# Splitting the last 1 KB of one key/value load unevenly, and joining four loads of output weights into two

## The chip, the cores and the metric

The kernel runs on one core of one Trainium2 chip. The metric is the time on the device in microseconds, of which the median over several executions is taken. A profile belongs to one execution; its span runs from the first to the last instruction of the program, and the execution's own time is a little longer.

## The reference

One decoding step for 8 sequences mixes two branches with a gate: `g * a + (1 - g) * b`, where `g = sigmoid(sum(x * gate_w))`.

Branch `a` is attention over the last 1024 positions of a cache, with 16 query heads over 8 key/value heads of 256 elements:

```
q = x @ wq                              # 8 x 4096, 16 heads of 256
p = softmax(q . k * 256**-0.5)          # each pair of query heads shares one key/value head
a = (p . v) @ wo                        # wo is 4096 x 448
```

Branch `b` is a layer norm, a matrix 448 x 1792 with bias and GELU, and a matrix 1792 x 448 with bias. All inputs are bfloat16. The keys and values of the window are by far the most of what has to be read: 16 groups of 2 MB each for the keys and as much for the values, out of 77.7 MB in all.

## The kernel before, in words

The cache is worked on in 16 groups (`NQ`), each of one sequence and four key/value heads. A group's keys are one tile of 128 partitions x 8192 elements (16 KB a partition, 2 MB in all), its values another. A partition holds 32 successive positions of one head, and partition `4 s + a` belongs to block `s` of positions and head `a` of the group. So the source of a load is a view of three dimensions: `s` (32), `a` (4), and the contiguous 8192 elements.

All large loads go through one ring of nine such tiles (`RING`), and all are issued by the SP queue. `plan` is the list of loads in their order: the query weights, the keys of group 0, the weights of branch `b`, then alternately keys of group `u` and values of group `u - 2` (`LAG`), the last two groups' values, and the output weights wo. `pump()` issues the next loads as soon as a ring tile is free, and `done()` says that one is. In the compiled program each load also waits on one of eight completion semaphores that are used in turn, which means that it waits for the load eight places before it.

wo is cut into four quarters of eight rows a partition. `WO_PARTS` says in which pieces each quarter is loaded: the first two quarters in two pieces of four rows (3584 B a partition, 448 KB), the last two in pieces of four, two and two rows. Two quarters share one ring tile. `project(q)` multiplies quarter `q` and waits for the pieces that it reads.

On the engines a group passes these steps. DVE turns the keys by 32 x 32 blocks (`turn_keys`, L358), PE forms the scores (`scores`, L430), DVE and ACT do the softmax (`top`, `share`, `expo`), DVE turns the weights (`turn`, L472), PE multiplies them with the values (`values`, L502), and `gather` and `finish` put the result into `oT`. The steps of three groups overlap in an order written out by hand. At the end come the last group's values, `spread_rows`, the four `project` calls (L673), one DVE instruction that adds the two branches (L691), and three small stores (L701).

Small inputs (`x_sb`, `gw_b`, both of eight rows, and the two biases) are loaded from the ACT queue at the start.

Of the kernel before, what the change touches and what calls it, by code (L numbers as in the profile page):

```python
# [18 lines left out]
def kernel(  # L19
# [15 lines left out]
    nc = tc.nc  # L35
# [3 lines left out]
    _, Hkv, Sk, Dh = A_k_cache.shape  # L39
# [20 lines left out]
    QUAD = 4  # L60
    RQ = QUAD * rep
    NQ = NB * Hkv // QUAD
    SK = P // QUAD
    NCK = W // SK
# [4 lines left out]
    HPQ = 4  # L69
    NHQ = Hq // HPQ  # L70
    NJ8 = HPQ * NJ
    WO_PARTS = [[(0, 4), (4, 8)]] * 2 + [[(0, 4), (4, 6), (6, 8)]] * 2
    RING = 9
    LAG = 2
    NK = 4
    NPAR = 2
    KP = NK * NPAR
    BLK = 32
# [10 lines left out]
    epool = ctx.enter_context(tc.tile_pool(name="epool", bufs=2))  # L89
    opool = ctx.enter_context(tc.tile_pool(name="opool", bufs=LAG + 1))  # L90
    ps_s = ctx.enter_context(tc.tile_pool(name="ps_s", bufs=2, space=PSUM))
# [18 lines left out]
    def kv_loader(src, u, parts):  # L110
        b, half = divmod(u, Hkv // QUAD)
        v = src[b, half * QUAD : (half + 1) * QUAD, kv_base:Sk, :].rearrange(
            "a (s c) d -> s a (c d)", c=NCK
        )

        def load(t):
            n = NCK * Dh // parts
            for i in range(parts):
                nc.sync.dma_start(
                    t[:, i * n : (i + 1) * n], v[:, :, i * n : (i + 1) * n]  # L120
                )

        return load

    def rows_loader(pieces):
        def load(t):
# [15 lines left out]
    def add(key, loader):  # L142
        index[key] = len(plan)
        plan.append(loader)

    def add_kv(name, src, u, parts=1):
        add((name, u), kv_loader(src, u, parts))
# [13 lines left out]
    for u in range(1, NQ):  # L161
        add_kv("k", A_k_cache, u)
        if u >= LAG:
            add_kv("v", A_v_cache, u - LAG)
    for u in range(NQ - LAG, NQ):
        add_kv("v", A_v_cache, u)
    for q in range(0, NHQ, 2):
# [5 lines left out]
                    for i in range(2)  # L173
                    for j0, j1 in WO_PARTS[q + i]
                ]
# [3 lines left out]
    def slot(*key):  # L179
        return slots[index[key]]  # L180
# [40 lines left out]
    qw = consts.tile([P, NJ, NU, AREA], BF16)  # L221
    pick = consts.tile([P, NK // NJ, NPAR, P], BF16)
    same = consts.tile([P, P], F32)
# [60 lines left out]
    )  # L284
    for kk in range(NK // NJ):
        for par in range(NPAR):
            nc.vector.tensor_copy(
                pick[:, kk, par, :].rearrange("p (b w) -> p b w", b=QUAD),
                ident[:]
                .rearrange("p (k o w r) -> p k r o w", k=NK // NJ, o=1, r=NPAR)[:, kk, par]  # L290
                .to_broadcast([P, QUAD, BLK]),
# [62 lines left out]
    def turn_keys(u, hf):  # L354
        kn = slot("k", u)
        kt = ktpool.tile([P, CH, NK, BLK, NPAR], BF16, tag="kt", name="kt")
        KT[u, hf] = kt
# [7 lines left out]
    def query():  # L365
# [31 lines left out]
        for j in range(NJ):  # L397
            for kk in range(NK // NJ):
                for par in range(NPAR):
# [19 lines left out]
    def scores(u, hf):  # L419
        if hf == 0:  # L420
            S[u] = ps_s.tile([P, W], F32, tag="S", name="S")
        cols = slice(hf * CH * BLK, (hf + 1) * CH * BLK)
        kt = KT.pop((u, hf))
        nc.tensor.matmul(  # L424
            S[u][:, cols], lhsT=foreign[:], rhs=place[:], start=True, stop=False
        )
        for k in range(NK):
            for par in range(NPAR):
                j, m = k // (NK // NJ), k % (NK // NJ) * NPAR + par
                nc.tensor.matmul(  # L430
                    S[u][:, cols],
                    lhsT=qw[:, j, u, m * RQ : m * RQ + P],
                    rhs=kt[:, :, k, :, par],
                    start=False,
                    stop=(k == NK - 1 and par == NPAR - 1),
                )
# [77 lines left out]
    def gather(u):  # L514
        first = soft.pop(u)
        os_ = epool.tile([P, Dh], F32, tag="os", name="os_")
        nc.vector.scalar_tensor_tensor(
            os_[:],
            in0=PO[:, 1, :],
            scalar=own[:, 1:2],  # L520
            in1=first[:],
            op0=ALU.mult,
            op1=ALU.add,
        )
        soft[u] = os_
# [89 lines left out]
    for u in range(1, NQ):  # L615
        turn_keys(u, 0)
        scores(u, 0)
        if u >= LAG + 1:
            gather(u - LAG - 1)
        if u >= LAG:  # L620
# [12 lines left out]
    u = NQ - 1  # L633
# [98 lines left out]
```

## Time and profile before

| | |
|---|---|
| median of 6 runs | 190.51 us (190.34 to 190.83) |
| the profiled execution's own time | 190.68 us |
| its span | 188.9 us |
| PE busy | 128.9 us, 68% |
| DVE busy | 127.9 us, 68% |
| ACT busy | 43.3 us, 23% |
| loads of keys and of values: one | 2 MB, 36.7 and 36.8 us from issue to landing (median) |
| loads of wo | 6 of 448 KB and 4 of 224 KB |
| read from memory | 77.68 MB, 411 GB/s over the span |

How to read the views that follow: the page's second part cuts the span into 40 slices of 4.7 us, with a digit for the busy tenths of each. Its third part counts the packets of each queue: q1 is SP's, q10 ACT's, q8 and q14 bring instructions. The chain of waits goes back from the last instruction to whatever released each step; its columns are start, length and what it was. A view of stretches gives, for each window, its length, the busy time and number of instructions of PE, PE's weight loads, DVE, ACT and POOL, the granted clock of PE, the DMA share and GB/s. The trace also has a record of each packet: its queue, size, start and duration.

### The profile page before, as it was taken

What the parts mean: (1) busy time and instruction counts of PE and PEld (TensorE: products, weight loads), DVE (VectorE), ACT (ScalarE), POOL (GpSimd) and SP (SyncE); (2) the same over time, 40 slices, a digit from 0 to 9 for tenths busy, and PEclk for the clock granted to TensorE, in tenths of its full rate; (3) what the DMA queues carried; (4) which work ended last, traced back from release to release, by engine and by line L of the source; (5) the groups of instructions that cost most, each with busy time, mean ns of one, the idle gap of its engine ahead of it and who ended that gap; (6) DMA issues with size and microseconds to landing.
All of it is one profiled execution on the core that took longest, in us unless ns stands there. A gap on an engine that the chain in (4) does not pass through costs nothing.

```text
span 188.9 us, 2411 instructions
## 1 busy us (share of the span) xinstructions
PE 128.9 (68%) x966; PEld 68.3 (36%) x975; DVE 127.9 (68%) x186; ACT 43.3 (23%) x91; POOL 5.0 (3%) x7
## 2 busy tenths in 40 slices
PE   0056879897847575786669675848399849687592
PEld 0022853442414242334225333323153514244281
DVE  7840488998949494949494949495868677785300
ACT  2032310034040404040404040404004310435200
POOL 8100000000000000000000000000000000000000
PEclk9999999999999999699979999999757987999558
DMA  6999999999999999999999999999999999999990
GB/s 213 408 427 427 434 433 429 430 430 427 437 430 427 427 437 427 427 430 441 427 430 425 434 427 434 434 427 434 423 434 434 437 420 434 427 437 415 409 375 28
DMA packets 7293, 77.84 MB, mean 412 GB/s; under 512 B 993, under 2 KB 1650, under 8 KB 2546
## 3 DMA queue, kind: packets, MB, share of 16 engines
q1 hardware_dynamic: 7088, 77.67, 97.0%
q8 instruction: 7, 0.11, 0.2%
q10 hardware_dynamic: 194, 0.02, 0.1%
q14 instruction: 4, 0.03, 0.0%
HBM read 77.68 MB, written 0.01 MB: 411 GB/s over the span
## 4 chain that ended last, share of the span: by engine, by line
DMA 79%; DVE 13%; PE 4%; ACT 2%; issue 1%; SPq 0%; ACTq 0%
DMA slot<-in_A_k_cache_dram 39%; DMA slot<-in_A_wo_dram 20%; DMA slot<-in_A_v_cache_dram 19%; DVE kt L358 5%; PE Sq L372 2%; DVE xz L246 1%; ACT qw L413 1%; DVE qw L415 1%; DVE mx L442 1%; PE qt L387 1%; ACT qs L382 1%; PE qp L400 1%; DVE Sq L199 0%; DVE ET L472 0%; PE gp L343 0%
## 5 line engine op out<-in xcount | busy, mean ns | idle before, releaser
L358 DVE STREAM_TRANSPOSE kt<-slot 128x2048 int32<-128x2048 int32 x32 | 73.7, 2305 | 31.5 <-DMA slot<-in_A_k_cache_dram 31.5
L430 PE MATMUL S<-kt,qw 128*128 128x512 bf16 x256 | 69.3, 417 | 35.2 <-DVE kt L358 30.5
L430 PEld LDWEIGHTS <-qw 128*128 128x128 bf16 x256 | 26.3, 103 | 72.2 <-issue 50.9
L459 ACT ACTIVATE E<-S,nmx 128x1024 bf16<-128x1024 f32 x16 | 22.2, 1388 | 2.8 <-DVE nmx L456 2.8
L535 ACT CAST oT<-fin 128x16 bf16<-128x16 f32 x16 | 3.6, 227 | 77.5 <-PE fin L532 77.5
L502 PE MATMUL PO<-slot,ET 128*16 128x512 bf16 x256 | 18.3, 410 | 1.2 <-DMA slot<-in_A_v_cache_dram 1.2
L442 DVE TENSOR_REDUCE mx<-S 128x1 f32<-128x1024 f32 x16 | 19.0, 1185 | 0.0
L511 ACT ACTIVATE first<-PO,own 128x256 f32<-128x256 f32 x16 | 7.6, 474 | 28.1 <-PE PO L502 26.7
L472 DVE STREAM_TRANSPOSE ET<-E 128x512 int32<-128x512 int32 x16 | 11.2, 698 | 2.2 <-ACT E L459 2.2
L424 PE MATMUL S<-place,foreign 128*128 128x512 bf16 x23 | 9.2, 400 | 0.2
L450 PE MATMUL mz<-m,same 128*128 128x4 f32 x32 | 6.2, 265 | 4.2 <-ACT oT L535 4.1
L483 PEld LDWEIGHTS den<-rowsum,rowden 128*128 128x128 f32 x32 | 6.7, 215 | 3.4 <-issue 1.1
L502 PEld LDWEIGHTS <-ET 128*16 128x16 bf16 x256 | 5.3, 91 | 5.8 <-issue 2.1
L450 PEld LDWEIGHTS mz<-m,same 128*128 128x128 f32 x32 | 5.0, 195 | 6.1 <-ACT oT L535 5.3
L424 PEld LDWEIGHTS <-foreign 128*128 128x128 bf16 x32 | 3.2, 100 | 8.5 <-issue 6.7
L483 PE MATMUL den<-rowsum,rowden 128*128 128x1 f32 x32 | 5.0, 226 | 0.4 <-ACT E L459 0.4
L673 PE MATMUL A_ps<-slot,oP 128*8 128x144 bf16 (+1 forms) x96 | 4.7, 316 | 0.7 <-DMA slot<-in_A_wo_dram 0.7
L415 DVE CAST qw<-qp 32x512 bf16<-32x512 f32 x4 | 2.7, 687 | 3.4 <-ACT qw L413 3.4
L494 ACT ACTIVATE rsel<-sel,rb 128x8 f32<-128x8 f32 x16 | 4.8, 297 | 1.1 <-DVE rb L493 1.1
L293 POOL MEMSET qw<- 128x5120 bf16 x1 | 4.4, 4366 | 0.0
L391 DVE COPY qd<-qt 128x64 bf16<-128x64 bf16 x4 | 0.6, 215 | 5.5 <-PE qt L387 5.5
L673 PEld LDWEIGHTS <-oP 128*8 128x8 bf16 x96 | 3.8, 114 | 1.2 <-issue 1.1
(135 smaller groups left out, 86.5 us busy)
## 6 DMA issues: line engine op xcount, KB each, us to landing
slot<-in_A_v_cache_dram SPq DMA_DIRECT2D x16, 2048.0 KB, 36.8
slot<-in_A_k_cache_dram SPq DMA_DIRECT2D x15, 2048.0 KB, 36.7
slot<-in_A_wo_dram SPq DMA_DIRECT2D x6, 448.0 KB, 31.3
slot<-in_A_wq_dram SPq DMA_DIRECT2D x1, 2048.0 KB, 7.7
slot<-in_A_k_cache_dram SPq DMA_DIRECT2D x2, 1024.0 KB
slot<-in_B_w_dram SPq DMA_DIRECT2D x1, 1568.0 KB
slot<-in_B_w_dram SPq DMA_DIRECT2D x1, 1344.0 KB, 11.8
slot<-in_A_wq_dram SPq DMA_DIRECT2D x1, 1024.0 KB
```

The lines of the kernel that those rows point to most:

```text
L358: nc.vector.transpose(kt[:].rearrange("p c k x r -> p (c k x r)").bitcast(WORD), kn[:, hf * CH * Dh : (hf + 1) * CH * Dh].bitcast(WORD),)
L424: nc.tensor.matmul(S[u][:, cols], lhsT=foreign[:], rhs=place[:], start=True, stop=False)
L430: nc.tensor.matmul(S[u][:, cols], lhsT=qw[:, j, u, m * RQ : m * RQ + P], rhs=kt[:, :, k, :, par], start=False, stop=(k == NK - 1 and par = ...
L442: nc.vector.reduce_max(mx[:], S[u][:], axis=AXIS.X)
L450: nc.tensor.matmul(mz[:], lhsT=same[:], rhs=m4[:], start=True, stop=True)
L459: nc.scalar.activation(E[:].rearrange("p c x i -> p c i x"), S.pop(u)[:].rearrange("p (c i x) -> p c i x", i=PAIR, x=BLK), ACT.Exp, bias=n ...
L472: nc.vector.transpose(ET[:].rearrange("p c r i -> p (c r i)").bitcast(WORD), E[:].rearrange("p c x i -> p (c x i)").bitcast(WORD),)
L483: nc.tensor.matmul(den[u][:], lhsT=rowden[:], rhs=rowsum[:], start=True, stop=True)
L494: nc.scalar.activation(rsel[u][:], sel2[:], ACT.Copy, scale=rb[:])
L502: nc.tensor.matmul(PO[32 * t : 32 * t + PAIR * RQ], lhsT=ET[:, c, 0:RQ, :], rhs=vn[:, PAIR * c * Dh : PAIR * (c + 1) * Dh], start=(c < QUA ...
L511: nc.scalar.activation(first[:], PO[:, 0, :], ACT.Copy, scale=own[:, 0:1])
L673: nc.tensor.matmul(dst, lhsT=oP[:, j, q, :], rhs=w[:, o + cols.start : o + cols.stop], start=(q == 0 and j == 0), stop=(q == NHQ - 1 and j ...
```

## The change

The values of group 6 are loaded in three transfers instead of one: the first 15 KB of each of the 128 rows, then the last 1 KB (`SKEW`, 512 elements) of the first 96 rows, then that of the other 32. The first two quarters of wo are loaded in one transfer each (7168 B a partition) instead of two. All the bytes, their places and the order of everything else stay as they are; no instruction of PE, DVE, ACT or POOL is added, removed or moved, and SP issues as many transfers as before, two more in the middle and two fewer at wo.

```diff
-    WO_PARTS = [[(0, 4), (4, 8)]] * 2 + [[(0, 4), (4, 6), (6, 8)]] * 2
+    WO_PARTS = [[(0, 8)]] * 2 + [[(0, 4), (4, 6), (6, 8)]] * 2
...
+    SKEW = 512
...
-        return load
+        def load_skewed(t):
+            n = NCK * Dh - SKEW
+            nc.sync.dma_start(t[:, :n], v[:, :, :n])
+            for s0, s1 in ((0, 24), (24, SK)):
+                nc.sync.dma_start(t[QUAD * s0 : QUAD * s1, n:], v[s0:s1, :, n:])
+
+        return load if parts else load_skewed
...
-            add_kv("v", A_v_cache, u - LAG)
+            add_kv("v", A_v_cache, u - LAG, parts=0 if u == NQ // 2 else 1)
```

## The prediction

> **What bounds the kernel now.** First the occupancy and transfer part of the page.
>
> ```profile
> DMA  6999999999999999999999999999999999999990
> GB/s 213 408 427 427 434 433 429 430 430 427 437 430 427 427 437 427 427 430 441 427 430 425 434 427 434 434 427 434 423 434 434 437 420 434 427 437 415 409 375 28
> DMA packets 7293, 77.84 MB, mean 412 GB/s; under 512 B 993, under 2 KB 1650, under 8 KB 2546
> ...
> q1 hardware_dynamic: 7088, 77.67, 97.0%
> q8 instruction: 7, 0.11, 0.2%
> ```
>
> The 16 DMA engines are busy from the second slice to the last but one, at about 430 GB/s, while PE and DVE are each busy 68% of the span. Then the chain of waits in order of time, at its end:
>
> ```profile
> 110.48 36.83 DMA slot<-in_A_v_cache_dram
> 147.31 0.02 issue
> 147.33 31.34 DMA slot<-in_A_wo_dram
> 178.67 0.02 issue
> 178.69 6.95 DMA slot<-in_A_wo_dram
> 185.64 0.04 issue
> 185.68 0.33 PE A_ps L673 x6
> 186.01 0.03 issue
> 186.04 0.38 DVE res L691
> ```
>
> Each link is a load whose landing frees the semaphore for the next one. The last part of wo lands at 185.64; after it come only six matmuls, one DVE instruction and the store. So the end is the moment when the slowest DMA engine has finished. Last, the stretches of 1 us around that moment (the last two columns are the DMA share and GB/s):
>
> ```profile
> 182.00:183.00 1.00, 1.00 (x32) 1.00 (x29) 0.29 (x1) 0.00 (x0) 0.00 (x0) 0.50 1.02 393
> 183.00:184.00 1.00, 1.00 (x22) 0.77 (x15) 0.00 (x0) 0.00 (x0) 0.00 (x0) 0.50 0.79 308
> 184.00:185.00 1.00, 0.44 (x12) 0.44 (x12) 0.00 (x0) 0.00 (x0) 0.00 (x0) 0.50 0.39 150
> 185.00:186.00 1.00, 0.81 (x18) 0.35 (x12) 0.00 (x0) 0.00 (x0) 0.00 (x0) 0.82 0.02 7
> ```
>
> The engines do not end together: 0.79, then 0.39 of 16 work on while the others are done. I followed the transfer records of the trace, where on one engine each packet starts where the one before ends. That gives 16 finishing times: nine engines end between 183.65 and 184.53, six between 184.98 and 185.35, one at 185.64; the mean is 184.52. The seven late ones are exactly those that each carried one of the seven 16 KB instruction packets of q8 (at 24.9, 43.4, 74.0, 102.6, 131.7, 160.7 and 180.6 us). Such a packet sets its engine back about 1.1 us: 0.61 of its own, and about 0.5 by which the rows beside it took longer. The engine that ends last got the last packet; the runner-up, at 185.35, the first.
>
> Which engines are these? The eight that carried the eight-row load of gw_b I call low, the rest high. The runner-up is low; the last one and the other five are high. One low, then six high is what a walk through engines 7, 8, ... 13 would give, so I place the last one at 13. That is an inference; the records carry no engine number.
>
> **What the Trainium skill says.** "DMA: Bandwidth & Descriptors", section on why a DMA increments its semaphore by 16: a transfer runs on the largest k up to 16 that divides the slowest dimension of both access patterns, on the lowest-numbered k engines. The trace agrees as far as it goes: 6272 rows, 16 completion writes for each of 49 loads, and twice 8 rows with 8 writes for the stores on SP, make 7088, the packets of q1. Applied to the change: the source of the 96 rows is 24 x 4 x 512, so k = 12, eight rows on each of engines 0 to 11; that of the 32 rows is 8 x 4 x 512, so k = 8, four rows on each of 0 to 7. No transfer before has k = 12.
> Same page, "Why small descriptors are slow": about 3 cycles are lost per packet. The records agree in size: a packet follows the next after 607 ns for 16 KB, 136 for 3584 B and 70 for 1792 B, which is 0.0368 ns per byte plus 4 ns; a completion write takes 6.
> Same page, "Bandwidth": transfers under 1 MB are inefficient. Here they are not, since they lie queued back to back: the 448 KB ones lose only these 4 ns per row.
>
> **The change part by part**, per DMA engine.
> - Values of group 6: 8 rows shrink by 1 KB each: -8 x 37.7 = -302 ns everywhere. The tail costs 41.7 ns a row and 6 ns per completion write: engines 0 to 7 get 12 rows and two writes, +512; 8 to 11 get 8 rows and one write, +340; 12 to 15 nothing.
> - wo: the first two quarters become 8 + 8 rows of 7168 B in place of 16 + 16 of 3584 B: 16 packets less, -64, and two writes less, -12.
> - Sum: engines 0 to 7 **+0.135 us**, 8 to 11 **-0.038**, 12 to 15 **-0.378**.
>
> New ends: the last one 185.64 - 0.38 = 185.26; the high ones in 8 to 11 at most 185.19 - 0.04 = 185.15; the low runner-up 185.35 + 0.13 = **185.49**, now last. The end moves by 185.49 - 185.64 = **-0.16 us** (-0.155 unrounded). The 0.74 us of PE and DVE and the store behind it stay.
>
> What I cost at nothing: SP issues two transfers more (about 0.53 us each) and two fewer of wo (0.33 each). Eight semaphores are shared in turn, so each transfer waits for the one eight before it; the tails take two of the eight places, and transfers behind them on SP are issued two loads later. The median issue-to-landing time is 36.8 us, about 7.6 loads of 4.86 us; it falls to some 27, still five loads ahead, so no engine runs dry. The last wo part is issued on the landing of the last values (176.5) instead of 178.67, earlier. From group 6 to wo the low engines run 0.21 us later (512 - 302), so keys and values land that much later: the matmuls on group 6 start at 100.99, 2.3 us after its landing at 98.69, which covers its own tail; at the end the matmuls on the last values, waiting for DMA at 176.5, shift by 0.21, and PE then sits idle 0.56 us before 184.56 for a wo part, which covers it. The single semaphore of quarter 0 comes with its second half, at 178.67 as before, and PE begins it only at 180.53; quarter 1 is whole at 180.87, needed at 181.67. If that cover were gone, PE would add at most the delay beyond it. DVE waits 31.5 us in all for keys, so 0.2 us is hidden there too; POOL and ACT's queue are not touched.
>
> The profiled execution took 190.68 us, its span 188.9; the median of the runs is 190.51, 0.17 lower. I take the difference off the median: 190.51 - 0.16 = **190.35**.
>
> **Rivals.** What a measurement can tell from no change is about 0.2%, 0.38 us.
> - *Full relief.* If in most executions the low engine with the instruction packet ends well ahead (its start and the cost of its packet vary), the relieved engine's whole 0.378 us counts: 190.13, right at the 0.2% line. For it: nothing else of the low eight is later than 184.53. Against: the runner-up is here only 0.29 behind.
> - *The last engine is one of 8 to 11*, or the late ones change places between executions: -0.04, 190.47. For it: the placing is inferred.
> - *Slower: the low engine is already last.* Place: the end of wo on the low engine with an instruction packet. Price +0.135 us, 190.65. It decides once that engine ends less than 0.135 us behind the last one; here it is 0.29. The tail can cost more than the sum if twelve engines are not used: 96 rows on eight engines would make it 16 rows on each low one, +0.30 us, 185.65 and 190.52.
> - *The skew does not come about.* If both tails spread over all 16 engines, each pays 32 + 12 ns for the tails and saves 76: -0.03, 190.48.
>
> **How the numbers follow.** Main case 0.48; full relief 0.15; last engine in 8 to 11 0.17; low engine last 0.09; no skew 0.11. All but full relief stay within 0.2%; of that, half lies beyond, and I add as much again for what I have not priced, in the rows beside the small packets or in the order of the late engines: faster by over 0.2% 0.16, within 0.2% 0.77, slower by over 0.2% 0.07 (the low case with a dearer tail). The range reaches from a little below full relief, 190.05, to a little above the low case, 190.72.
>
> **What would show it.** q1 should hold 6948 packets: 7088 - 256 + 128 rows, and 32 - 20 completion writes less; with tails on all 16 engines it would be 6960. Packets under 512 B should fall from 993 to 981 (993 without skew). In the stretches around the end, the DMA share should fall to nothing some 0.16 us earlier, and the landing of the last wo part, 185.64, with it. I am wrong if the keys' waits on DVE grow by more than about 0.2 us each, if the DMA share dips after group 6, or if PE waits for quarter 0 or 1 of wo and not for the last part.

## The result: slower by a quarter of a per cent

The changed kernel takes 190.95 us (median of 20 runs, 190.64 to 191.48), the kernel before 190.48 (40 runs beside it). The ratio is 1.0025, 95% interval 1.0015 to 1.0034: +0.47 us where -0.16 was forecast. (The ratios here leave out single executions that stand far above the rest.) The profiled execution took 191.30 us, its span 189.5.

The occupancy and transfer part of the page of the changed kernel:

```profile
DMA  6999999999999999999999999999999999999990
GB/s 212 416 420 436 435 422 437 429 425 432 425 439 429 429 429 429 439 429 425 429 398 384 431 436 436 422 432 432 425 436 429 432 429 432 432 425 428 412 380 29
DMA packets 7153, 77.84 MB, mean 411 GB/s; under 512 B 981, under 2 KB 1766, under 8 KB 2406
...
q1 hardware_dynamic: 6948, 77.67, 97.1%
```

The packets are those forecast for 12 and 8 engines: 6948 on q1, and 981 under 512 B. The new thing is in the GB/s row: slices 21 and 22 (about 95 to 104 us) show 398 and 384 where the row of before had nothing below 420 between its third and its 36th slice. The DMA row keeps its nines there. So the engines don't run dry; they are busy for longer with the same bytes.

The end of the chain of waits:

```profile
177.25 0.02 issue
177.27 8.99 DMA slot<-in_A_wo_dram
186.26 0.04 issue
186.30 0.33 PE A_ps L680 x5
186.63 0.03 issue
186.66 0.38 DVE res L698
```

The last part of wo is issued at 177.27, earlier than before, as forecast, and still lands at 186.26 in place of 185.64. Six matmuls (the chain lists five of them, the trace has six), one DVE instruction and the store follow as before. The whole difference is in the landing.

The stretches of 1 us around it, with the same columns as before:

```profile
183.00:184.00 1.00, 1.00 (x32) 1.00 (x26) 0.05 (x1) 0.00 (x0) 0.00 (x0) 0.50 1.04 410
184.00:185.00 1.00, 0.76 (x16) 0.53 (x10) 0.00 (x0) 0.00 (x0) 0.00 (x0) 0.50 0.69 266
185.00:186.00 1.00, 0.64 (x18) 0.44 (x18) 0.00 (x0) 0.00 (x0) 0.00 (x0) 0.85 0.20 77
186.00:187.00 1.00, 0.39 (x12) 0.10 (x5) 0.34 (x1) 0.00 (x0) 0.00 (x0) 1.00 0.00 0
```

The DMA share falls over two stretches as before, half to one us later: the engines are late together, not one of them. Where they lost the time is seen when longer stretches are laid around the two low slices. First the kernel before, then the changed one:

```profile
85.00:97.00 12.00, 6.73 (x44) 3.43 (x45) 9.23 (x11) 2.26 (x5) 0.00 (x0) 0.98 1.01 434
97.00:100.00 3.00, 3.00 (x11) 1.71 (x9) 2.96 (x4) 0.00 (x0) 0.00 (x0) 0.50 1.01 431
100.00:103.00 3.00, 2.68 (x26) 1.37 (x26) 0.95 (x3) 1.15 (x4) 0.00 (x0) 0.99 0.99 421
103.00:115.00 12.00, 7.42 (x48) 3.56 (x47) 8.66 (x9) 3.33 (x7) 0.00 (x0) 1.00 1.01 431
```

```profile
85.00:97.00 12.00, 6.77 (x44) 3.43 (x45) 9.20 (x11) 2.25 (x5) 0.00 (x0) 0.98 1.01 431
97.00:100.00 3.00, 3.00 (x11) 1.71 (x9) 2.96 (x4) 0.00 (x0) 0.00 (x0) 0.51 1.03 378
100.00:103.00 3.00, 2.68 (x26) 1.33 (x26) 0.91 (x3) 1.16 (x4) 0.00 (x0) 1.00 0.98 366
103.00:115.00 12.00, 9.07 (x47) 4.05 (x47) 7.92 (x9) 3.30 (x7) 0.00 (x0) 0.86 1.01 429
```

For six microseconds 372 GB/s on average flow in place of 426, with PE, DVE and ACT doing the same work as before. The packet records give the detail; their times count here and below from the same zero as the views (the prediction put them 0.35 us later, so that the last one meets its landing at 185.64). The two tails, the transfers of 96 and of 32 rows of 1 KB, pass between 96.1 and 98.5 us. The slow 16 KB rows start between 96.6 and 102.8 us. They settle at 707 ns on every one of the 16 engines, also on those that carry no tail; before and after that a row takes 611, but for the rows beside an instruction packet. Added up and divided by 16, an engine loses 0.80 us there.

The engine that waits for these rows shows it too. DVE turns the keys of group 9, first before, then in the changed kernel:

```profile
103.57 2.31 DVE L358 STREAM_TRANSPOSE kt<-slot 128x2048 int32<-128x2048 int32 x1 [2.32 <-DMA slot<-in_A_k_cache_dram]
```

```profile
104.47 2.31 DVE L365 STREAM_TRANSPOSE kt<-slot 128x2048 int32<-128x2048 int32 x1 [3.25 <-DMA slot<-in_A_k_cache_dram]
```

The wait is 0.93 us longer, and all such waits together are 33.2 us in place of 31.5.

### The profile page after: what moved, and what is told of

Its sections match the earlier page's. It is cut to its first block, busy times and chain, and to the rows that moved or that the text cites. A ratio compares the mean times of both kernels' runs of the same rounds, so it can differ in the third digit from the quotient of the medians.

```text
span 189.5 us, 2411 instructions
## 1 busy us (share of the span) xinstructions
PE 129.1 (68%) x966; PEld 68.3 (36%) x975; DVE 128.1 (68%) x186; ACT 43.3 (23%) x91; POOL 5.0 (3%) x7
## 3 DMA queue, kind: packets, MB, share of 16 engines
q1 hardware_dynamic: 6948, 77.67, 97.1%
## 4 chain that ended last, share of the span: by engine, by line
DMA 91%; DVE 5%; PE 2%; issue 0%; SPq 0%
DMA slot<-in_A_k_cache_dram 57%; DMA slot<-in_A_v_cache_dram 19%; DMA slot<-in_B_w_dram 6%; DMA slot<-in_A_wo_dram 5%; DMA slot<-in_A_wq_dram 4%; DVE kt L365 4%; PE S L437 2%; DVE mx L449 1%; DVE ET L479 0%; DVE res L698 0%; DVE os__1181 L524 0%; PE A_ps L680 0%; DVE m L451 0%; PE den L490 0%; SPq L120 0%
## 5 line engine op out<-in xcount | busy, mean ns | idle before, releaser
L365 DVE STREAM_TRANSPOSE kt<-slot 128x2048 int32<-128x2048 int32 x32 | 73.7, 2305 | 33.3 <-DMA slot<-in_A_k_cache_dram 33.2
L451 DVE TENSOR_SCALAR m<-block,mx 128x4 f32<-128x4 f32 x16 | 3.7, 229 | 0.6
```

The source lines that it names most:

```text
L365: nc.vector.transpose(kt[:].rearrange("p c k x r -> p (c k x r)").bitcast(WORD), kn[:, hf * CH * Dh : (hf + 1) * CH * Dh].bitcast(WORD),)
```

## The experiments

The first four runs weigh three theories, which the expectations call by number: 1, transfers on fewer than 16 engines make the load behind them slow; 2, it is the two more transfers or the rows of 1 KB as such; 3, it is the joined loads of wo. The later ones weigh theory A, transfers over fewer than 128 rows disturb the stream (A1: because fewer than 16 engines are used, A2: because of the rows alone), against theory B, there are too few large loads in flight. All edits are to the kernel before, with constants written out; "lost" is the packets' time above the usual one of their size, from the records of the traced execution, per engine.

**One part at a time.** `skew_only` leaves the edit of `WO_PARTS` out, `wo_only` makes that edit alone:

```diff
-    WO_PARTS = [[(0, 4), (4, 8)]] * 2 + [[(0, 4), (4, 6), (6, 8)]] * 2
+    WO_PARTS = [[(0, 8)]] * 2 + [[(0, 4), (4, 6), (6, 8)]] * 2
```

> Only the split of the values of group 6 (15 KB rows, then 96 and 32 rows of 1 KB); wo is loaded as in the kernel before. Theory 1 (transfers that run on fewer than 16 DMA engines make the load behind them slow): the 16 KB rows of the keys of group 9 take about 707 ns in place of 611 on all engines, 8 x 96 = 0.77 us each, and the time is 0.4 to 0.7 us above before, 190.9 to 191.2. Theory 2 (two more transfers in the eight places, or rows of 1 KB as such): the same here. Theory 3 (the joined loads of wo are to blame): within 0.1 us of before, 190.4 to 190.6, and no slow rows.

> Only the first two quarters of wo in one transfer each. Theories 1 and 2: 16 packets and two completion writes less on each engine, -0.08 us, 190.4, no slow rows anywhere. Theory 3: slower by 0.3 us or more.

The split alone takes 1.0054 times as long (1.0033 to 1.0075), 191.65 us; wo alone 1.0006 (0.9998 to 1.0014), which is no difference that can be told. Theory 3 is out. The gain of 0.08 us that I had for wo doesn't show either. The stretches of the split alone, 97 to 100 and 100 to 103 us:

```profile
97.00:100.00 3.00, 2.70 (x16) 1.51 (x13) 2.90 (x3) 0.23 (x1) 0.00 (x0) 0.98 1.00 361
100.00:103.00 3.00, 2.98 (x26) 1.39 (x27) 0.88 (x3) 1.55 (x3) 0.00 (x0) 1.00 1.00 360
```

Here the rows settle at 732 ns, and 0.98 us are lost.

**Tails over all engines.** In the split's loader:

```diff
-            for s0, s1 in ((0, 24), (24, SK)):
+            for s0, s1 in ((0, 16), (16, SK)):     # tail_64_64
+            for s0, s1 in ((0, SK),):              # tail_128
```

> As the split alone, but the tails have 64 and 64 rows (source 16 x 4 x 512 each), so that both run on 16 engines by the rule of the skill: the same number of transfers, the same bytes, no skew. Theory 1: no slow rows, time +0.04 us (8 packets of 4 ns and 2 writes of 6 ns per engine), 190.5. Theory 2: the keys of group 9 slow as in the changed kernel, 190.9 to 191.2.

> As the split alone, but the tail is one transfer of 128 rows of 1 KB on 16 engines. Theory 1: no slow rows, 190.5. Theory 2 by number of transfers: about half the loss, 190.7; by the 1 KB rows: 190.9 to 191.2.

`tail_128`: ratio 1.0012 (0.9999 to 1.0024), no slow rows, 437 and 418 GB/s in the two stretches. So rows of 1 KB do no harm. `tail_64_64`: ratio 1.0027 (1.0013 to 1.0041), with times from 190.63 to 191.52; the traced execution, at 190.63, has a few rows of 630 to 675 ns at its tails and had lost only 0.04 us. As first put, theory 1 (fewer than 16 engines) did not foresee that the kernel is slower; so I took a second trace of it.

> The same kernel as tail_64_64, for a second execution's trace. If its times of 190.6 to 191.5 come from slow rows that appear in some executions only, an execution of 191 or more shows them here, and one of 190.7 does not.

This execution took 205.78 us. Its row of GB/s, and stretches from 85 us on:

```profile
GB/s 233 401 429 436 439 419 427 440 414 447 427 424 437 424 440 427 427 433 425 376 368 360 360 360 360 360 363 363 360 360 360 360 360 357 360 360 360 373 396 39
```

```profile
85.00:97.00 12.00, 7.93 (x51) 3.93 (x51) 9.20 (x12) 2.25 (x5) 0.00 (x0) 1.00 1.00 424
97.00:100.00 3.00, 2.68 (x29) 1.65 (x27) 2.96 (x3) 0.23 (x1) 0.00 (x0) 1.00 1.09 406
100.00:110.00 10.00, 5.78 (x22) 2.16 (x19) 6.13 (x9) 2.00 (x4) 0.00 (x0) 0.75 1.00 360
110.00:140.00 30.00, 21.95 (x116) 10.90 (x117) 15.93 (x20) 6.66 (x15) 0.00 (x0) 0.74 1.01 360
140.00:170.00 30.00, 21.08 (x120) 10.29 (x119) 20.68 (x24) 4.75 (x12) 0.00 (x0) 0.83 1.01 360
```

The fall begins as the two tails pass (96.2 to 98.3 us) and does not end: 732 ns a row to the last 16 KB row, 15.0 us lost on these rows. PE's granted clock was 1.00 as it began, so it does not come from there. The tails themselves are two microseconds long. So they don't make particular rows slow; they set off a slower way in which the stream runs, here at 360 GB/s, and it keeps it for a time that differs from one execution to the next.

Single executions of other kernels with narrow transfers are long too: 204.40 us (`skew_only`), and of the kernels further below 194.41 (`skew_group2`), 194.34 and 199.67 (`extra_96_k16`) and four between 194.05 and 200.78 (`skew_first_keys`). They have no trace. Of 189 executions of the kernel before, and of 66 of the four changed kernels whose stream has no narrow transfer, none took more than 192.04.

This long execution also shows what kind of limit it is. Three 16 KB instruction packets, each on one engine, pass in the slow stream, at 100.2, 136.9 and 171.8 us. For about a microsecond the rows of the other engines take some 694 ns instead of 732, and then 732 again. In the kernel before, they keep their 611 ns as such a packet passes. A limit on the sum of all 16 engines would give 732 x 15/16 = 686 ns, by estimate; a slowing of each engine by itself would give no change. So in the slow stream the engines seem to share one limit, and at 611 ns each has its own. That is an inference from these lengths.

**Loads in flight, place, one narrow transfer.** `tail_128_twice` cuts the last 1 KB into two transfers of 128 rows; `skew_group2` puts the uneven split on group 2; `extra_96` keeps the loads and adds a transfer into an unused tile:

```diff
+            for o in (n, n + SKEW // 2):                                             # tail_128_twice
+                nc.sync.dma_start(t[:, o : o + SKEW // 2], v[:, :, o : o + SKEW // 2])
...
+            add_kv("v", A_v_cache, u - LAG, parts=0 if u == NQ // 4 else 1)          # skew_group2
...
+            nc.sync.dma_start(t[:], v)                                               # extra_96
+            nc.sync.dma_start(extra[0:96, :], v[0:24, :, NCK * Dh - 304 :])
```

> The values of group 6 in 15 KB rows and then two transfers of 512 B rows, each over all 128 rows; wo as before. As many transfers as with the uneven split, so as few large loads in flight (five to six in place of seven to eight when group 9's keys arrive), but no narrow transfer. Theory A (transfers over fewer than 128 rows disturb the load behind them): no slow rows, 190.5 to 190.65. Theory B (too few loads in flight): slow rows in the keys of group 9, median 190.8 to 191.6.

> The uneven split (96 and 32 rows) put on the values of group 2 in place of group 6; wo as before. Both theories: the slow rows move with it, to the load behind it, the keys of group 5, at about 58 to 64 us, and the time is 190.9 to 191.7. If the loss belongs to that place (what the other engines do at 97 us), it is gone: 190.4 to 190.6.

> The kernel before plus one extra transfer behind the values of group 6: 96 rows of 608 B of the same values into an unused tile (k = 12 by the rule of the skill). One narrow transfer, and only one place in flight lost. Theory A: slow rows in the keys of group 9, 190.9 or more. Theory B: as with one tail of 128 rows, none or hardly any; +0.2 us on engines 0 to 11 for 8 rows of about 26 ns, 190.5 to 190.7.

`tail_128_twice`, with as many transfers as the uneven split, has no slow rows in its trace:

```profile
97.00:100.00 3.00, 2.69 (x12) 1.42 (x10) 2.96 (x3) 0.23 (x1) 0.00 (x0) 0.74 1.06 448
100.00:103.00 3.00, 3.00 (x26) 1.39 (x27) 0.59 (x3) 1.56 (x3) 0.00 (x0) 1.00 1.00 426
```

Theory B is out as the cause of the slow rows; the kernel is still 1.0014 slower (1.0004 to 1.0024), more than the 0.1 us that its packets cost. `skew_group2` (1.0039, 1.0013 to 1.0065) has them where its tails pass, at 57.2 to 59.5 us, and not at 97:

```profile
46.00:57.00 11.00, 5.95 (x41) 3.09 (x42) 8.26 (x10) 2.26 (x5) 0.00 (x0) 1.00 1.01 434
57.00:60.00 3.00, 2.96 (x8) 1.20 (x8) 2.96 (x5) 0.00 (x0) 0.00 (x0) 0.56 1.01 373
60.00:63.00 3.00, 2.68 (x26) 1.72 (x26) 1.77 (x3) 0.29 (x2) 0.00 (x0) 0.87 1.01 431
```

In this execution the slow rows ended with the tails (0.33 us lost, 190.72 us). `extra_96` (1.0038, 1.0021 to 1.0055) shows that one narrow transfer is enough: slow rows that start between 96.9 and 100.3 us and settle at 700 ns.

**Fewer engines or fewer rows?** `extra_96_k16` takes its 96 rows from wo, in a view of two dimensions; `extra_128` is the control.

```diff
-            nc.sync.dma_start(extra[0:96, :], v[0:24, :, NCK * Dh - 304 :])
+            nc.sync.dma_start(extra[0:96, :], wo_v[0:96, 0, 0:304])                  # extra_96_k16
+            nc.sync.dma_start(extra[0:128, :], v[0:32, :, NCK * Dh - 304 :])         # extra_128
```

> As the kernel with one extra transfer of 96 rows, but its source is 96 rows of wo, a view of two dimensions, so that by the rule of the skill it runs on all 16 engines, six rows each (q1: 16 completion writes more than before, not 12). Theory A1 (fewer than 16 engines is what disturbs): no slow rows, 190.45 to 190.6. Theory A2 (fewer than 128 rows is what disturbs[...]): slow rows in the keys of group 9, 190.8 or more.

> The control: the extra transfer with 128 rows of the values, 16 engines. Both theories: no slow rows; 8 packets of 26 ns and a write, +0.2 us, 190.6 to 190.7.

> A second trace of the kernel with 96 extra rows over all 16 engines. If fewer than 128 rows are enough to start the slow stretch, slow rows from about 98 us and a time of 191 or more; if fewer than 16 engines are needed, none and 190.6 to 190.9.

On q1 there are 7196 packets for the 96 rows of values and 7200 for those of wo: 12 and 16 completion writes, as the rule has it. `extra_128` has no slow rows (1.0020, 1.0007 to 1.0032). `extra_96_k16` (1.0020, 1.0005 to 1.0034) had but two longer rows in its first trace. In the second, at 190.87 us, it had a milder stretch, with rows of up to 684 ns and 0.20 us lost; the stretches from 97 us on:

```profile
97.00:100.00 3.00, 2.68 (x29) 1.73 (x27) 2.96 (x4) 0.23 (x1) 0.00 (x0) 1.00 1.01 429
100.00:103.00 3.00, 2.72 (x18) 0.97 (x11) 0.75 (x3) 2.02 (x4) 0.00 (x0) 1.00 1.05 412
```

But these rows start at 100.4 us, two microseconds after the extra transfer had passed (96.4 to 98.4 us), so this trace ties them to it less firmly; and the control has as large a ratio. The case against "fewer than 16 engines" rests on `tail_64_64`, where each engine carries four rows of each tail: slow rows at the tails in both traces, in one of them to the end of the stream. So fewer than 16 engines isn't needed, and neither is an uneven share of the engines. Whether either makes the slow stretch likelier is left open: all seven traces in which a transfer used 12 engines in the middle of the stream or near its end have slow rows, of the four traces with 64 or 96 rows over 16 engines two clearly. What it is about a narrow transfer, the number of its rows or where they go, no run separates.

**Other places for the split.** `skew_last_values` puts it on the last group's values, `skew_first_keys` on the second half of the keys of group 0.

> The uneven split on the values of the last group, so that parts of wo lie behind it and no 16 KB rows; wo as before. If the disturbance lasts for the load behind the narrow transfers alone: short rows of wo are slow instead, 448 KB at most, a loss below 0.2 us, and the skew's gain of up to 0.16 shows: 190.3 to 190.5. If it lasts for some microseconds whatever lies behind: 190.8 to 191.3.

> The kernel before with the uneven split on the second half of the keys of group 0 (7 KB rows, then 96 and 32 rows of 1 KB), so that the narrow transfers pass at about 18 us. If the slow stretch needs the steady stream of 16 KB rows: no slow rows, and the skew's own gain shows, 190.3 to 190.5. If narrow transfers start it anywhere: slow rows from about 18 us on, 190.8 or more.

`skew_last_values` (1.0036, 1.0023 to 1.0049) has 390 GB/s between 176 and 179 us, as its tails end (174.0 to 176.3 us), where the kernel before has 418. Of 301 rows of wo of 3584 B between 174 and 178 us 124 take over 150 ns, where the kernel before takes 140 for each, and 0.32 us are lost: being near the end doesn't help. `skew_first_keys` (1.0036, 1.0016 to 1.0057) had no slow 16 KB rows in its trace, since none were near; but as its tails passed, at 15.6 to 16.6 us, 29 rows of 10.5 KB took 427 to 622 ns, where all such rows of the kernel before take 404, and 0.18 us were lost. So the slow rows need no stream of 16 KB rows, and with single executions of up to 200.78 us the start is no safe place either. Its traced execution, at 191.93 us, ended in another way, on PE; the end of its chain:

```profile
181.59 1.02 PE fin L535 x4
182.61 1.16 PE A_ps L676 x23
183.77 0.14 PE pp L660 x14
183.91 3.20 PE A_ps L676 x61
187.11 0.03 issue
187.13 0.38 DVE res L694
```

Here PE reached the output weights some 2 us later than in the trace of before and no longer waited for them. The traces of `tail_128_twice` (191.87 us) and `extra_96` (192.05) ended so too. That is a second loss, beside the slow rows, and its cause was not looked for; the kernel before also has single times of 191.5 to 192, without a trace of them.

**How long it lasts in the changed kernel.** Two more traces of it:

> The changed kernel once more, for another trace. If a slow stretch of rows (700 to 735 ns) starts with the narrow transfers and lasts a random time, it starts at about 97 us again and ends elsewhere; the time above 190.35 is about 0.16 times its length.

> A third trace of the changed kernel, with the same expectation: slow rows from about 97 us on, for a time that differs between executions, and a total that grows by about 0.16 of that time.

| changed kernel | slow rows, us | lost per engine | time | time less the loss |
|---|---|---|---|---|
| first trace | 96.6 to 102.8 | 0.80 us | 191.30 | 190.50 |
| again | 96.5 to 98.7 | 0.34 us | 190.80 | 190.46 |
| third | 97.1 to 103.3 | 0.78 us | 191.62 | 190.84 |

The second column says when the slow rows start. In the third trace they settle at 682 ns. All three stretches begin with the tails, and they end at different times. The spread of the 20 runs (0.84 us) is about twice that of these three losses.

The ends are not without order. In the first and third trace, in `skew_only` and in `extra_96` the slow rows hold one length until a 16 KB instruction packet starts, at 102.6, 103.3, 102.7 and 100.1 us. The last slow row starts within 0.3 us of that, and the next take 611 ns. In the second trace and in `skew_group2` the slow rows end with the tails, before any such packet. And the long execution let three packets pass. So such a packet may end the stretch, but is neither needed for it nor always enough; no run tried it by itself.

## Why the prediction was wrong

- **What bounds the kernel** was read rightly for these traces: the slowest DMA engine sets the end. That is also why the loss comes through: 0.80 us on all engines in the changed kernel, 15.0 us in the long execution. That a gain of 0.1 us comes through as well is not shown.
- **How the rows are shared out** was right: the packet counts are those of 12 and 8 engines, as the Trainium skill's page "DMA: Bandwidth & Descriptors" has it in its section on why a DMA increments its semaphore by 16. In the trace a 1 KB packet takes 46 ns, and the next follows after 42: 41.7 was used.
- **The step that failed** is the sum under "The change part by part" and the "New ends" made from it. It prices the packets of the tails and of wo alone, and so puts at nothing, without a reason, what the tails do to the rows of the loads behind them, which were to keep their 607 ns from one row to the next. They are some 70 to 120 ns longer for a while, on all 16 engines, and cost 0.34 to 0.80 us in the three traces of the changed kernel, more than the 0.16 that was to be gained. In the first of them the sum is 190.68 - 0.16 + 0.80 = 191.32, and it took 191.30. That it fits so closely is luck: the three traces of the table leave 190.46 to 190.84, which does not show that the skew gains 0.16.
- **The waits** for wo were harmless as said: its last part was issued early, and PE waited for the last parts and not for quarter 0 or 1. The loads in flight are not the cause either, by `tail_128_twice`. One sign that I had named for being wrong did show: a wait of DVE for keys grew by more than 0.2 us, that for group 9, by 0.93.
- **The skew's own gain** is not seen in any kernel. Whether the engine that ends last in the changed kernel is one of the four relieved ones, as the prediction inferred, the traces don't settle, since the packet records carry no engine number.
- **wo**: forecast -0.08 us, measured 1.0006 with an interval that holds -0.02% to +0.14%: no gain to be seen.
- **The rivals and the range**: I named "the rows beside the small packets" as something not priced, and gave it and the order of the late engines some 0.08 of chance, all on the side of a gain; the 0.07 for a loss was for dearer tails. Such an effect had never been seen in the trace of before, which has no transfer of this shape in the stream, so nothing there bounded its sign or its size. I should have allowed for it on the slow side too, by some tenths of a microsecond for one load that runs at a lower rate, and not by the packets alone. I also said that the DMA share would dip if I was wrong. It doesn't: slow packets count as busy, and only GB/s shows them.

How a narrow transfer makes the stream run slower is not shown. The runs show what starts it, that it takes all engines alike, and that its length differs between executions.

## What to carry to other kernels

In a kernel whose end is set by a saturated stream of loads, try to keep every transfer of the stream on all 128 rows: 128 KB moved by narrow transfers cost more here, by the rows around them, than the imbalance that they were to mend. Read GB/s beside the DMA share, since an engine that is slowed is still busy. And where a mean of several executions moves with a wide spread, take more than one trace before believing in a size.

## What the runs showed of the hardware that was not expected

The stream of 16 KB rows runs at 611 ns a row on each engine, some 430 GB/s in all, or for a while slower, with rows that settle at 680 to 732 ns, down to 360 GB/s. Narrow transfers (96 and 32 rows, 96 alone, 64 and 64) set off the slow stretch; in one execution it held from 97 us to the end of the 16 KB rows, 205.78 us in all. Transfers over 128 rows, of 512 B to 16 KB a row, did so in none of five traces. In the slow stream the other engines get faster while one carries an instruction packet, 694 in place of 732 ns, so they seem to share one limit there. And in the trace of before each 16 KB packet of instructions set the one engine that carries it back by about 1.1 us, and the seven engines that carried one ended last.
